# A gated mix of two attentions: x taken in features-first from the host instead of being transposed on TensorE

## The chip, the core and the metric

The kernel runs on one core of a Trainium2 chip. The metric is the device time of one execution in microseconds (us). A difference of about 0.5% (10 us here) is what a measurement of this kernel can tell from no change.

## The reference, cut to what matters

```
x: 2048 x 512                                     # float32, one batch
g = sigmoid((x * gate_w).sum(-1))                 # one number per row of x
qA, kA, vA = x @ wq, x @ wk, x @ wv               # 32 heads of 16
qB, kB, vB = split(x @ wqkv)                      # 32 heads of 16
a = (local attention in 4 segments of 512 rows, causal,
     mixed by sigmoid(beta) with a linear-attention memory carried over the segments) @ wo
b = softmax(qB kB' / 4) vB @ B_wo                 # over all 2048 rows
out = g * a + (1 - g) * b
```

x is an operand of all six projections, which contract over its 512 features. TensorE contracts over partitions, so the projections need x with features on the partitions. Only the gate needs x with rows on the partitions.

## The kernel before, in words

The 2048 rows are cut into four chunks of 512 rows, and each chunk into four tiles of 128 rows. Each float32 operand of a projection is split into a rounded part ("hi", the tiles `xh`, `ws`, `wv`) on ScalarE and a rest ("lo", `xl`) on VectorE, and a projection of a tile or chunk is three products of four 128-deep matmuls each, 12 matmuls into one PSUM bank (`TERMS`, L253).

**The start (L642 to L686).** SyncE loads x in 16 tiles of 128 rows, 256 KB each, into an eight-slot buffer `RAW` (`load_x`, L159). `do_x` (L163) transposes a tile in four 128x128 pieces on TensorE, copies the PSUM bank to `xh` on ScalarE (L171), and subtracts on VectorE into `xl` (L172). `dot_gate` (L177) multiplies the same rows by `gate_w` on VectorE and sums them. Then come eight jobs `qk_job` (L274), two for each chunk: queries and keys of attention B for the first group of eight heads. A job ends with a copy on ScalarE (L286), a subtraction on VectorE (L289) and two stores of 256 KB each to DRAM on SyncE's queue (L295), whose DRAM side has the shape 8 x 16 x 512; the staging tile `st` has four buffers. The transposes of the next chunk stand between a chunk's first and second job in TensorE's order.

**The A value projection (L686 to L700).** Sixteen jobs `v_job("A", tt)` (L255), one for each row tile. ScalarE copies each result (L267) into one of two staging tiles `VS` that lie in `vb` and hold two jobs each; SyncE stores a staging tile when it is full (L269, 544 KB, 128 partitions wide: the "value stores" below, eight of them). Jobs 5 and 6 therefore wait for value store 1, jobs 9 and 10 for value store 3, and so on. PSUM has six banks in rotation here, so TensorE's job n needs the copy of job n - 6. Between the second and the third value store SyncE issues twelve loads of `beta`, which fetch single 4-byte elements (L184, L187). GpSimd's own queue loads weights (L234, L242) and fills constant rows from a tile `aux` in 256-byte pieces (L148) during this time. `do_gate` (L198) takes the sigmoid of the gate sums.

**The rest.** Sixteen blocks of A's query and key projections with the memory, the B value projection as filler (L722 to L805), then 32 iterations of scores, exponentials and products with the values (L905 to L939), and a tail.

Every engine works its instructions strictly in the order of the program text (`manual_schedule`, L43). The order on a DMA queue is the order of issue. SyncE's DMAs share eight semaphores in turn, so a DMA is issued only when the one issued eight places before it has landed.

Of the kernel before, what the change touches and what calls it, by code (L numbers as in the profile page):

```python
# [7 lines left out]
FT = mybir.dt.float32  # L8
# [3 lines left out]
AF = mybir.ActivationFunctionType  # L12
OP = mybir.AluOpType
# [5 lines left out]
E = 16  # L19
SEQ = 2048  # L20
DM = 512
C = 512
NC4 = SEQ // C
NT = SEQ // 128
# [6 lines left out]


@with_exitstack
def gated_mix_kernel(ctx, tc, x, wq, wk, wv, wo, beta, wqkv, wob, gate_w, out):
    nc = tc.nc
    xr = x.rearrange("b s d -> (b s) d")
    outr = out.rearrange("b s d -> (b s) d")
# [13 lines left out]
    ident = P.tile([128, 128], FT, name="ident")  # L51
# [19 lines left out]
    X = proj.enter_context(tc.tile_pool(name="proj", bufs=1))  # L71
    XL = [X.tile([128, 4, C], FR, name=f"xl{c}") for c in range(NC4)]
# [22 lines left out]
    def misc():  # L95
        return bank(mode["misc"])
# [12 lines left out]
    def rot(key, lst):  # L109
        i = cnt.get(key, 0)  # L110
        cnt[key] = i + 1
        return lst[i % len(lst)]

    def raw_buf():
        i = cnt.get("raw", 0)
        cnt["raw"] = i + 1
        return RAWV[i if i < 6 else 6 + (i - 6) % 8]


    def identity():  # L120
        jp = X.tile([128, C], FT, name="phi0").bitcast(I32)[:, :128]
        nc.gpsimd.iota(jp, pattern=[[1, 128]], base=0, channel_multiplier=-1)
        nc.vector.tensor_scalar(ident, jp, 0.0, None, op0=OP.is_equal)

        for j in range(2):
            r = slice(64 * j, 64 * j + 64)
            for n in range(2):
                o = 64.0 * (n - j)
                nc.vector.tensor_scalar(crows[r, n], jp[r], o, None, op0=OP.is_equal)
                nc.vector.tensor_scalar(cmask[r, n], jp[r], o, MASK, op0=OP.is_gt, op1=OP.mult)  # L130

    def constants():
# [21 lines left out]
    def load_gate():  # L154
        nc.sync.dma_start(gw, bass.AP(tensor=gate_w.tensor, offset=gate_w.offset, ap=[[0, 128], [1, DM]]))

    XR = {}

    def load_x(tt):  # L159
        XR[tt] = RAW[:, tt % 8]  # L160
        nc.sync.dma_start(XR[tt], xr[tt * 128:(tt + 1) * 128, :])

    def do_x(tt):  # L163
        c, tl = divmod(tt, 4)
        xt = XR.pop(tt)
        b = misc().rearrange("p (k t) -> p k t", k=4)
        for k in range(4):
            nc.tensor.transpose(b[:, k, :], xt[:, k * 128:(k + 1) * 128], ident)
        hi = XH[c][:, :, tl * 128:(tl + 1) * 128]
        lo = XL[c][:, :, tl * 128:(tl + 1) * 128]  # L170
        nc.scalar.activation(hi, b, AF.Copy)  # L171
        nc.vector.tensor_tensor(lo, b, hi, op=OP.subtract)  # L172
        XG[tt] = xt

    XG = {}

    def dot_gate(tt):  # L177
        scr = W.tile([128, DM], BF, name="scr", bufs=1)
        nc.vector.scalar_tensor_tensor(scr, XG.pop(tt), 1.0, gw, op0=OP.mult, op1=OP.mult,
                                       accum_out=gate[:, tt:tt + 1])  # L180
# [17 lines left out]
    def do_gate():  # L198
        e = X.tile([128, NT], FT, name="ge")
        nc.scalar.activation(e, gate, AF.Exp, scale=-1.0)  # L200
        nc.vector.tensor_scalar(e, e, 1.0, None, op0=OP.add)
        nc.vector.reciprocal(gate, e)
# [17 lines left out]
    def split(hi, lo, raw):  # L220
        nc.scalar.activation(hi, raw, AF.Copy)
        nc.vector.tensor_tensor(lo, raw, hi, op=OP.subtract)

    def wcols(kd, w):
        if kd == "A":
            return (wq, wk, wv)[w], 0
        return wqkv, w * DM

    WR = {}

    def load_wv(kd, k):
        src, c0 = wcols(kd, 2)
        WR[k] = raw_buf()
        nc.gpsimd.dma_start(WR[k], src[k * 128:(k + 1) * 128, c0:c0 + DM])  # L234

    def split_wv(k):
        split(WV[0][:, k, :], WV[1][:, k, :], WR.pop(k))

    def load_w_raw(kd, g, w):
        src, c0 = wcols(kd, w)  # L240
        raw = raw_buf().rearrange("p (k c) -> p k c", k=4)
        nc.gpsimd.dma_start(raw, src.rearrange("(k p) c -> p k c", p=128)[:, :, c0 + g * 128:c0 + (g + 1) * 128])  # L242
        return raw

    def load_w(kd, g):
        WR[kd, g] = [load_w_raw(kd, g, w) for w in range(2)]

    def split_w(n, kd, g, ws=(0, 1)):
        for w in ws:
            split(WS[n][w][0], WS[n][w][1], WR[kd, g][w])  # L250
# [4 lines left out]
    def v_job(kd, tt):  # L255
        c, tl = divmod(tt, 4)
        b = misc()
        n = 0
        for xi, wi in TERMS:
            for k in range(4):  # L260
                lhs = (XH, XL)[xi][c][:, k, tl * 128:(tl + 1) * 128]
                nc.tensor.matmul(b, lhs, WV[wi][:, k, :], start=n == 0, stop=n == 11)  # L262
                n += 1
        if tl % 2 == 0:
            rot("vs", VS)
        vs = VS[(cnt["vs"] - 1) % 2]
        nc.scalar.activation(vs[:, tl % 2, :, :E], b.rearrange("p (h e) -> p h e", h=H), AF.Copy)  # L267
        if tl % 2:
            nc.sync.dma_start(VD[kd][tt * 128 - 128:(tt + 1) * 128].rearrange("(a t) g h e -> t a (g h e)", a=2),  # L269
                              vs.rearrange("p a h e -> p a (h e)"))  # L270
# [70 lines left out]
    def load_vm(g, c):  # L341
        PHI[g, "v", c] = X.tile([128, 4, 8, E + 1], FT, name="vm", bufs=2)
        v_src(PHI[g, "v", c], "A", g, c)
# [37 lines left out]
    def load_q(u):  # L381
        kd, qd, c = UN[u]
        load_qk(q_of(u), kd, 0, qd, c)
# [249 lines left out]
    def todo(fn, *a):  # L633
        return lambda: fn(*a)
# [4 lines left out]
    def s_tasks(u):  # L639
        return [todo(s_a, u, *t) for t in ST_A] if u < 32 else [todo(s_b, u, *t) for t in ST_B]  # L640

    for tt in range(4):  # L642
        load_x(tt)
    identity()
    load_w("B", 0)
    for tt in range(4, 8):
        load_x(tt)
    load_gate()
    constants()

    for tt in range(3):
        do_x(tt)
    split_w(0, "B", 0, (0,))
    do_x(3)
    split_w(0, "B", 0, (1,))
    def dots(tt):
        for t in (tt, tt + 1):
            dot_gate(t)
            if t + 8 < NT:
                load_x(t + 8)  # L660

    dots(0)
    dots(2)
    for c in range(NC4):
        for w in range(2):
            qk_job(0, "B", 0, w, c)
            if c + 1 < NC4:
                if w == 0:
                    for t in range(4):
                        do_x(4 * c + 4 + t)  # L670
                dots(4 * c + 4 + 2 * w)
            elif w == 0:
                split_wv(3)
        if c == 1:
            for k in range(4):
                load_wv("A", k)
        if c == 2:
            for k in range(3):
                split_wv(k)
# [5 lines left out]
        nc.vector.memset(t.bitcast(FT), 0.0)  # L685
    for tt in range(NT):  # L686
        v_job("A", tt)
        if tt == 2:
            split_w(0, "A", 0)
            do_gate()  # L690
        if tt == 3:
            load_beta()
        if tt in (7, 9, 11):
            load_wv("B", (tt - 7) // 2)
        if tt == NT - 1:
            load_vm(0, 0)
            load_kb(0)
            load_q(32)
        if ax:
            set_aux(*ax.pop(0))  # L700
# [21 lines left out]
    for blk in range(16):  # L722
        g, c = divmod(blk, 4)
# [9 lines left out]
        n = blk + 1 + (c == 2)  # L733
# [261 lines left out]
```

## Time and profile before

| | |
|---|---|
| device time, three runs | 1976.98, 1983.9 and 1985.88 us; median 1983.9 |
| the profiled execution | span 1976.0 us from first to last instruction; its own time is not listed apart, the lowest of the three runs is 1.0 us above the span |
| TensorE (PE) busy | 98% of the span |
| VectorE (DVE) busy | 83% |
| ScalarE (ACT) busy | 73% |
| GpSimd (POOL) busy | 13% |

Busy time counts an engine's instructions, not the waits between them. PEld is the weight load of a matmul, SPq the instruction by which SyncE issues a DMA, POOL with a DMA instruction the same on GpSimd's queue. A row of a timeline has the start in us from the begin of the span, the duration of the group, the engine, the line, the operation with its output and inputs, and in brackets how long the engine had been idle and what ended that. "PEclk" is the share of its clock that TensorE was granted. q1 is the queue of the DMAs that SyncE issues, q0 that of GpSimd's.

### The profile page before, as it was taken

What the parts mean: (1) busy time and instruction counts of PE and PEld (TensorE: products, weight loads), DVE (VectorE), ACT (ScalarE), POOL (GpSimd) and SP (SyncE); (2) the same over time, 40 slices, a digit from 0 to 9 for tenths busy, and PEclk for the clock granted to TensorE, in tenths of its full rate; (3) what the DMA queues carried; (4) which work ended last, traced back from release to release, by engine and by line L of the source; (5) the groups of instructions that cost most, each with busy time, mean ns of one, the idle gap of its engine ahead of it and who ended that gap; (6) DMA issues with size and microseconds to landing.
All of it is one profiled execution on the core that took longest, in us unless ns stands there. A gap on an engine that the chain in (4) does not pass through costs nothing.

```text
span 1976.0 us, 43643 instructions
## 1 busy us (share of the span) xinstructions
PE 1944.8 (98%) x17517; PEld 945.6 (48%) x17517; DVE 1630.3 (83%) x1825; ACT 1435.7 (73%) x2703; POOL 257.5 (13%) x474
## 2 busy tenths in 40 slices
PE   8999999999999999999999999999999999999999
PEld 6887777434344344444444444444444444444435
DVE  6135665899999999999999999999999999999942
ACT  3233332688888888888888888888888888888884
POOL 2200000011210101111010101010101010101012
PEclk9999999999999999999999999999999999999999
DMA  6766656644443444344445353444344444444111
GB/s 205 172 209 183 191 186 173 152 111 114 97 114 88 103 86 103 86 114 86 114 85 112 86 113 86 114 86 114 86 108 91 96 102 87 102 90 103 48 51 57
DMA packets 162742, 222.49 MB, mean 113 GB/s; under 512 B 39260, under 2 KB 89452, under 8 KB 156780
## 3 DMA queue, kind: packets, MB, share of 16 engines
q1 hardware_dynamic: 159596, 211.70, 44.0%
q0 software_dynamic: 2944, 8.00, 2.1%
q8 instruction: 138, 2.26, 0.5%
q14 instruction: 64, 0.52, 0.1%
HBM read 148.21 MB, written 68.16 MB: 109 GB/s over the span
## 4 chain that ended last, share of the span: by engine, by line
PE 90%; DMA 3%; DVE 2%; ACT 2%; issue 1%; SPq 1%; ACTq 0%; DVEq 0%
PE pvb L525 31%; PE tb L503 17%; PE sbk L449 12%; PE mb L503 8%; PE tb L279 3%; PE tb L591 2%; PE mb L279 2%; PE sbk L427 2%; PE pvb L279 2%; PE tb L262 2%; DVE mxb L451 1%; ACT raw L509 1%; PE mb L591 1%; PE mb L262 1%; PE sbk L431 1%
## 5 line engine op out<-in xcount | busy, mean ns | idle before, releaser
L451 DVE TENSOR_REDUCE mxb<-sbk 128x2 f32<-128x1024 f32 x1024 | 1226.1, 1222 | 36.6 <-PE sbk L449 32.4
L509 ACT ACTIVATE raw<-tb 128x512 f32<-128x512 f32 x1557 | 888.2, 598 | 163.1 <-PE tb L503 90.7
L525 PE MATMUL pvb<-raw,vb 128*17 128x256 f32 (+1 forms) x8072 | 639.4, 388 | 0.0
L509 ACT ACTIVATE raw<-mb 128x512 f32<-128x512 f32 x780 | 466.4, 598 | 76.5 <-PE tb L503 44.8
L503 PE MATMUL tb<-qb,xh 64*128 64x512 f32 x872 | 330.8, 496 | 1.7 <-ACT raw L509 1.7
L525 PEld LDWEIGHTS pvb<-raw,vb 128*17 128x17 f32 x8072 | 134.4, 95 | 341.7 <-issue 336.6
L449 PE MATMUL sbk<-xh,qb 64*128 64x512 f32 x1344 | 283.1, 398 | 2.0 <-DMA xh<-dB 0.8
L503 PE MATMUL mb<-qb,xh 64*128 64x512 f32 x445 | 219.6, 494 | 0.0
L503 PEld LDWEIGHTS tb<-qb,xh 64*128 64x128 f32 x872 | 124.4, 183 | 188.1 <-issue 91.4
L512 POOL TENSOR_SCALAR_AFFINE_SELECT raw<-raw 128x256 f32<-128x256 f32 (+1 forms) x320 | 116.1, 363 | 700.1 <-ACT raw L509 692.3
L503 PE MATMUL tb<-qb,kb 64*128 64x512 f32 x471 | 176.3, 496 | 1.4 <-DMA qb<-mr 0.8
L435 DVE TENSOR_REDUCE mx<-sbk 128x2 f32<-128x768 f32 (+1 forms) x128 | 139.8, 1092 | 43.1 <-PE sbk L431 37.1
L449 PE MATMUL sbk<-kb,qb 64*128 64x512 f32 x704 | 150.6, 406 | 1.2 <-DVE mxb L451 1.1
L449 PEld LDWEIGHTS sbk<-xh,qb 64*128 64x128 f32 x1344 | 137.9, 186 | 7.3 <-DVE mxb L451 3.5
L503 PEld LDWEIGHTS mb<-qb,xh 64*128 64x128 f32 x445 | 81.3, 183 | 86.6 <-issue 48.0
L503 PE MATMUL mb<-qb,kb 64*128 64x512 f32 x233 | 115.4, 495 | 0.7 <-DVE st L289 0.7
L565 POOL TENSOR_TENSOR o<-o,d 128x512 f32<-128x512 f32 x31 | 39.8, 1283 | 562.6 <-DMA d<-rd 281.6
L503 PEld LDWEIGHTS tb<-qb,kb 64*128 64x128 f32 x471 | 66.0, 183 | 98.4 <-issue 52.5
L525 PE MATMUL pvb<-raw,va 128*17 128x256 f32 (+2 forms) x1280 | 94.7, 383 | 5.8 <-ACT pvs L534 5.8
L427 PE MATMUL sbk<-ka,qa 64*128 64x256 f32 (+3 forms) x512 | 86.8, 346 | 1.2 <-ACT raw L509 1.2
L503 PE MATMUL tb<-qa,ka 64*128 64x384 f32 (+3 forms) x340 | 79.2, 372 | 0.0
L449 PEld LDWEIGHTS sbk<-kb,qb 64*128 64x128 f32 x704 | 71.6, 185 | 12.6 <-issue 6.5
(273 smaller groups left out, 1790.7 us busy)
## 6 DMA issues: line engine op xcount, KB each, us to landing
xh<-dB SPq DMA_DIRECT2D x38, 512.0 KB
vb<-vdB SPq DMA_DIRECT2D x16, 1088.0 KB
dB<-st SPq DMA_DIRECT2D x64, 256.0 KB
dA<-st SPq DMA_DIRECT2D x64, 256.0 KB
pd<-pvs SPq DMA_DIRECT2D x64, 256.0 KB
kb<-dB SPq DMA_DIRECT2D x22, 512.0 KB
xh<-dB SPq DMA_DIRECT2D x38, 256.0 KB
qb<-dB SPq DMA_DIRECT2D x64, 128.0 KB
```

What stands on the lines that cost most here:

```text
L262: nc.tensor.matmul(b, lhs, WV[wi][:, k, :], start=n == 0, stop=n == 11)
L279: nc.tensor.matmul(b, WS[ws][w][wi][:, k, :], (XH, XL)[xi][c][:, k, :], start=n == 0, stop=n == 11)
L427: nc.tensor.matmul(b[:, j, c0:c0 + n], q_of(u)[r, p, i * 128:(i + 1) * 128], k_of(u, p)[r, :n], start=True, stop=False)
L435: nc.vector.tensor_reduce(m[:, :, p, i], b[:, :, :n], axis=AX.X, op=OP.max)
L449: nc.tensor.matmul(b[:, j], q_of(u)[r, p, i * 128:(i + 1) * 128], k_of(u, p)[r, kc * C:(kc + 1) * C], start=True, stop=True)
L451: nc.vector.tensor_reduce(MXB[u][:, :, p, i, kc], b, axis=AX.X, op=OP.max)
L503: nc.tensor.matmul(bs[j][:, c0:c0 + w], k_of(u, h // 2)[r, 128 * it:128 * it + 128], q_of(u)[r, h // 2, q0:], start=True, stop=True)
L509: nc.scalar.activation(pt, bs[j], AF.Exp, scale=SCALE)
L512: nc.gpsimd.affine_select(out=m, in_=m, pattern=[[1, 128]] if n < 2 else [[0, 2], [1, 128]], compare_op=OP.is_ge, fill=0.0, base=0, channe ...
L525: nc.tensor.matmul(PVB[32 * h:32 * h + E + 1, q0 + lo:q0 + hi], vt[:, it, 4 * q + h, :], pt[:, lo:hi], start=it == 0 and lo == 0, stop=it ...
L565: nc.gpsimd.tensor_tensor(o, o, d, op=OP.mult)
L591: nc.tensor.matmul(b, (AT["oh"], AT["ol"])[oi][:, g, a], (AT["wh"], AT["wl"])[wi][:, g, a], start=n == 0, stop=n == 11)
```

## The change

The host also hands over x with features first (`xt`, 512 x 2048). The kernel loads a chunk of it as `[128 features, 4, 512 rows]`, 1 MB, into one half of `RAW`; chunk 0 in four DMAs of 256 KB, each later chunk in one. The split goes from SBUF: ScalarE copies `RAW` to `xh`, VectorE subtracts to `xl`. The 64 transposes and their 16 visits of a PSUM bank are gone from TensorE.

The rows of x are still loaded, for the gate alone, into four tiles whose names are otherwise used later (`phi0`, `phi1`, `om`, `pk`), one row tile per load, each load after the sum of the tile four places before it. Rows 0 to 3 are issued after the load of chunk 2, rows 4 to 9 one by one after the stores of jobs 3 to 8, row 10 ahead of the first value store, rows 11 and 12 behind it, 13 behind the second, 14 behind the `beta` loads, 15 behind the third; `do_gate` moves from job 3 to job 11 there. The load of chunk 3 comes after the stores of job 1. The load of the query weights of the first job goes to ScalarE's queue, that of the key weights stays on GpSimd's. The constants on VectorE and the identity come after the first loads.

```
-    def do_x(tt):
-        c, tl = divmod(tt, 4)
-        xt = XR.pop(tt)
-        b = misc().rearrange("p (k t) -> p k t", k=4)
-        for k in range(4):
-            nc.tensor.transpose(b[:, k, :], xt[:, k * 128:(k + 1) * 128], ident)
-        hi = XH[c][:, :, tl * 128:(tl + 1) * 128]
-        lo = XL[c][:, :, tl * 128:(tl + 1) * 128]
-        nc.scalar.activation(hi, b, AF.Copy)
-        nc.vector.tensor_tensor(lo, b, hi, op=OP.subtract)
-        XG[tt] = xt
+    XS = [RAW[:, 4 * (c % 2):4 * (c % 2) + 4] for c in range(NC4)]
+
+    def load_xt(c, ks=slice(0, 4)):
+        nc.sync.dma_start(XS[c][:, ks], xt.rearrange("(k p) t -> p k t", p=128)[:, ks, c * C:(c + 1) * C])
+
+    def split_x(c, ks):
+        split(XH[c][:, ks], XL[c][:, ks], XS[c][:, ks])
+
     def load_x(tt):
-        XR[tt] = RAW[:, tt % 8]
-        nc.sync.dma_start(XR[tt], xr[tt * 128:(tt + 1) * 128, :])
+        t = X.tile(*(([128, C], FT), ([128, C], FT), ([128, 4, 8, E], FT), ([128, 4, 128], FT))[tt % 4],
+                   name=("phi0", "phi1", "om", "pk")[tt % 4])
+        XG[tt] = t if tt % 4 < 2 else t.rearrange("p i h e -> p (i h e)" if tt % 4 == 2 else "p i r -> p (i r)")
+        nc.sync.dma_start(XG[tt], xr[tt * 128:(tt + 1) * 128, :])
...
+    WR["B", 0] = [load_w_raw("B", 0, w, (nc.scalar, nc.gpsimd)[w]) for w in range(2)]
+    for k in range(4):
+        load_xt(0, slice(k, k + 1))
+    load_xt(1)
+    load_gate()
+    identity()
+    split_w(0, "B", 0, (0,))
+    for k in range(4):
+        split_x(0, slice(k, k + 1))
+    split_w(0, "B", 0, (1,))
+    load_xt(2)
+    for tt in range(4):
+        load_x(tt)
+    constants()
...
+    def dot(tt):
+        if 0 <= tt < NT:
+            dot_gate(tt)
+            if tt + 4 < NT:
+                load_x(tt + 4)
+
     for c in range(NC4):
         for w in range(2):
             qk_job(0, "B", 0, w, c)
             if c + 1 < NC4:
                 if w == 0:
-                    for t in range(4):
-                        do_x(4 * c + 4 + t)
-                dots(4 * c + 4 + 2 * w)
+                    for n in range(2):
+                        split_x(c + 1, slice(2 * n, 2 * n + 2))
+                    if c == 0:
+                        load_xt(3)
             elif w == 0:
                 split_wv(3)
+            dot(2 * c + w - 2)
...
     for tt in range(NT):
         v_job("A", tt)
+        dot(tt + 6)
         if tt == 2:
             split_w(0, "A", 0)
+        if tt == 10:
             do_gate()
```

`split` is the helper that the weights already used (L220): one ScalarE copy, one VectorE subtraction.

More of the change, by code (lines that the diff above doesn't have):

```diff
@@ L33, in gated_mix_kernel @@
 @with_exitstack
-def gated_mix_kernel(ctx, tc, x, wq, wk, wv, wo, beta, wqkv, wob, gate_w, out):
+def gated_mix_kernel(ctx, tc, x, wq, wk, wv, wo, beta, wqkv, wob, gate_w, xt, out):
     nc = tc.nc
@@ L155, in load_gate @@
         nc.sync.dma_start(gw, bass.AP(tensor=gate_w.tensor, offset=gate_w.offset, ap=[[0, 128], [1, DM]]))
-    XR = {}
-    def load_x(tt):
-        XR[tt] = RAW[:, tt % 8]
-        nc.sync.dma_start(XR[tt], xr[tt * 128:(tt + 1) * 128, :])
-    def do_x(tt):
-        c, tl = divmod(tt, 4)
-        xt = XR.pop(tt)
-        b = misc().rearrange("p (k t) -> p k t", k=4)
-        for k in range(4):
-            nc.tensor.transpose(b[:, k, :], xt[:, k * 128:(k + 1) * 128], ident)
-        hi = XH[c][:, :, tl * 128:(tl + 1) * 128]
-        lo = XL[c][:, :, tl * 128:(tl + 1) * 128]
-        nc.scalar.activation(hi, b, AF.Copy)
-        nc.vector.tensor_tensor(lo, b, hi, op=OP.subtract)
-        XG[tt] = xt
-    XG = {}
+    XS = [RAW[:, 4 * (c % 2):4 * (c % 2) + 4] for c in range(NC4)]
[3 more added lines that the diff above has]
+        split(XH[c][:, ks], XL[c][:, ks], XS[c][:, ks])
+    XG = {}
+    def load_x(tt):
+        t = X.tile(*(([128, C], FT), ([128, C], FT), ([128, 4, 8, E], FT), ([128, 4, 128], FT))[tt % 4],
+                   name=("phi0", "phi1", "om", "pk")[tt % 4])
+        XG[tt] = t if tt % 4 < 2 else t.rearrange("p i h e -> p (i h e)" if tt % 4 == 2 else "p i r -> p (i r)")
+        nc.sync.dma_start(XG[tt], xr[tt * 128:(tt + 1) * 128, :])
     def dot_gate(tt):
@@ L237, in split_wv, with load_w_raw @@
         split(WV[0][:, k, :], WV[1][:, k, :], WR.pop(k))
-    def load_w_raw(kd, g, w):
+    def load_w_raw(kd, g, w, eng=None):
         src, c0 = wcols(kd, w)
         raw = raw_buf().rearrange("p (k c) -> p k c", k=4)
-        nc.gpsimd.dma_start(raw, src.rearrange("(k p) c -> p k c", p=128)[:, :, c0 + g * 128:c0 + (g + 1) * 128])
+        (eng or nc.gpsimd).dma_start(raw, src.rearrange("(k p) c -> p k c", p=128)[:, :, c0 + g * 128:c0 + (g + 1) * 128])
         return raw
@@ L640, in s_tasks @@
         return [todo(s_a, u, *t) for t in ST_A] if u < 32 else [todo(s_b, u, *t) for t in ST_B]
+    WR["B", 0] = [load_w_raw("B", 0, w, (nc.scalar, nc.gpsimd)[w]) for w in range(2)]
[9 more added lines that the diff above has]
+    load_xt(2)
     for tt in range(4):
         load_x(tt)
[L644 to L648, printed above, removed]
-    constants()
[L651 to L663, printed above, removed]
+    constants()
+    def dot(tt):
[3 more added lines that the diff above has]
+                load_x(tt + 4)
     for c in range(NC4):
@@ L986 @@
         args.append(nc.dram_tensor(f"in_{name}_dram", a.shape, _mybir.dt.from_np(a.dtype), kind="ExternalInput").ap())
+    a = _np.ascontiguousarray(inputs["A_x"][0].T)
+    arrays["in_xt_dram"] = a
+    args.append(nc.dram_tensor("in_xt_dram", a.shape, _mybir.dt.from_np(a.dtype), kind="ExternalInput").ap())
     for i, (shape, dtype) in enumerate(_OUTS):
```

## The prediction

> **What bounds the kernel now.** I read the page first, then the busy time by stage, then the start and the value projection row by row, last the DMA queues.
>
> ```profile
> span 1976.0 us, 43643 instructions
> ...
> PE 1944.8 (98%) x17517; PEld 945.6 (48%) x17517; DVE 1630.3 (83%) x1825; ACT 1435.7 (73%) x2703; POOL 257.5 (13%) x474
> ...
> PE 90%; DMA 3%; DVE 2%; ACT 2%; issue 1%; SPq 1%; ACTq 0%; DVEq 0%
> ```
>
> TensorE fills 98% of the span and 90% of the chain that ended last. Each engine works in a fixed order, so a microsecond that TensorE saves early arrives at the end, if nothing takes it back on the way.
>
> ```profile
> core 0: us, PE busy (x) PEld busy (x) DVE busy (x) ACT busy (x) POOL busy (x), PEclk, DMA share, GB/s
> 0.00:10.30 10.30, 4.14 (x16) 3.00 (x16) 4.81 (x15) 4.21 (x7) 6.33 (x19) 1.00 0.81 272
> 10.30:43.90 33.60, 30.95 (x144) 25.36 (x145) 25.55 (x58) 12.87 (x24) 0.22 (x1) 0.95 0.60 192
> 43.90:88.60 44.70, 44.70 (x195) 36.31 (x194) 4.81 (x8) 8.73 (x17) 17.08 (x31) 1.00 0.74 162
> ```
>
> The change lies in the first two stages, ahead of 43.9 us. The third, the A value projection, keeps TensorE full (44.70 of 44.70); after it the code is the same. So the question is when TensorE leaves the third stage. (About 0.5%, 10 us, is what a measurement of this kernel can tell from no change.)
>
> ```profile
> ACT vb L267 <- DMA vdA<-vb: 27.1, 6, 13.9
> ...
> PEld mb L262 <- ACT vb L267: 0.2, 1, 0.2
> ```
>
> These two waits say that it only just stays full: ScalarE's copies wait 27.1 us for value stores to land, and once TensorE itself waits for such a copy.
>
> ```profile
> 65.64 1.09 ACT L267 ACTIVATE vb<-sbk 128x512 f32<-128x512 f32 x2 [8.34 <-DMA vdA<-vb]
> ...
> 82.26 0.60 ACT L267 ACTIVATE vb<-mb 128x512 f32<-128x512 f32 x1 [13.91 <-DMA vdA<-vb]
> ...
> 82.95 1.38 PE L262 MATMUL mb<-wv,xh 128*128 128x512 f32 x5
> ```
>
> This is the place: the copy of job 9 waits until 82.26 for the third value store, and TensorE's job 15, which needs that PSUM bank, starts at 82.95, 39.05 us after the stage began. All six banks are used up: **any later landing of the third store, measured from the stage's start, stops TensorE**.
>
> **The change part by part.**
>
> ```profile
> 10.33 3.66 PE L279 MATMUL sbk<-xh,ws 128*128 128x512 f32 x8 [0.69 <-ACT xh L171]
> 13.83 1.09 PE L279 MATMUL sbk<-xl,ws 128*128 128x512 f32 x4
> 14.76 0.60 PE L168 MATMUL sbk<-ident,raw 128*128 128x128 f32 x4
> ...
> 16.42 2.10 PE L279 MATMUL pvb<-xh,ws 128*128 128x512 f32 x8
> ...
> 19.28 2.02 PE L279 MATMUL sbk<-xh,ws 128*128 128x512 f32 x8
> ...
> 33.05 0.66 PE L168 MATMUL tb<-ident,raw 128*128 128x128 f32 x4 [2.63 <-DMA raw<-in_A_x_dram]
> ...
> 34.12 3.66 PE L279 MATMUL pvb<-xh,ws 128*128 128x512 f32 x8
> ```
>
> *Removed.* Four tiles of transposes take 1.66 us of TensorE (14.76 to 16.42), three chunks' worth 5.0 us; a wait of 2.6 us for rows of x and the slow clock behind it (8 matmuls in 3.66 us instead of 2.02, so 1.64 us) go too. A job of 12 matmuls takes 2.8 us (16.42 to 19.28).
>
> ```profile
> 8.49 0.60 ACT L171 ACTIVATE xh<-mb 128x512 fp32r<-128x512 f32 x1 [2.34 <-PE mb L168]
> ...
> 8.99 0.62 ACT L221 ACTIVATE ws<-va 128x512 fp32r<-128x512 f32 x1
> ...
> 9.73 0.68 DVE L222 TENSOR_TENSOR ws<-va,ws 128x512 fp32r<-128x512 f32 x1
> ...
> 14.44 0.69 DVE L179 SCALAR_TENSOR_TENSOR scr<-raw,gw 128x512 bf16<-128x512 f32 x1 [2.82 <-DMA gw<-in_gate_w_dram]
> ```
>
> ```profile
> 3.50:8.50 5.00, 3.06 (x12) 2.29 (x12) 1.49 (x3) 1.20 (x3) 3.86 (x12) 1.00 0.96 328
> ```
>
> *Chunk 0.* Four loads and two weights are the same bytes as now, so the fourth piece lands at about 8.5; split from SBUF by rows of this kind, 0.62 and 0.68 us, its lo is there at 9.8. Job 1 does eight of its matmuls by then, and with the slow clock ends near 12.6, against 14.9. Without any wait the other seven would end at 12.6 + 7 x 2.8 = 32.
>
> *Chunk 3 comes late.* The load of chunk 2 joins the queue behind `gate_w` (landed 14.4). Behind it stand rows 0 to 3, job 1's stores, and only then chunk 3. At 328 GB/s a megabyte takes 3.2 us: 14.4 + 3.2 + 3.2, stores with their constant 3.4 (rate below), + 3.2 = 27.4. Half a split more, at most 1.24 on ScalarE: job 7 starts near 28.5 instead of 26.6, and the value stage starts at **about 34** instead of 43.9. So TensorE is 9.6 us ahead there (bounds 7 to 12: chunk 3 three later, or no wait).
>
> *Moving the query weights to ScalarE's queue* I cost at nothing: the sum of bytes ahead of chunk 0 is what it was. Bounds: 0.6 us either way, the 0.62 of one split. The gate sums on VectorE keep their number (16 x 0.69) and have cover: VectorE is busy 4.81 of 44.7 us in the value stage.
>
> *What takes the gain back: the queue.* x is now read twice, 4.2 MB more, and the copies of rows stand in SyncE's queue among the stores.
>
> ```profile
> q1 hardware_dynamic: 821, 1.56, 51.6%
> ...
> dB<-st SPq DMA_DIRECT2D x4, 256.0 KB
> ```
>
> ```profile
> 14.00:16.00 2.00, 2.00 (x16) 1.78 (x16) 1.50 (x5) 1.04 (x3) 0.00 (x0) 1.00 0.00 0
> 16.00:38.00 22.00, 19.37 (x97) 15.87 (x95) 18.30 (x41) 8.04 (x16) 0.00 (x0) 0.92 0.66 203
> 38.00:44.00 6.00, 6.00 (x28) 4.85 (x27) 4.54 (x10) 3.29 (x6) 0.22 (x1) 1.00 0.45 146
> ```
>
> The first fence is the queue from 30 to 38 us, where it holds only jobs' stores: its share stands at half, 1.56 MB in 8 us, 195 GB/s. I read this as eight of the sixteen DMA engines full and eight idle. A store of 0.26 MB then takes 1.34 us of those eight. A row tile, spread over all sixteen, takes them half of 1.34, **0.67 us**.
>
> By the Trainium skill, "DMA: Bandwidth & Descriptors", section "Why a DMA increments its semaphore by 16 and not by 1", a DMA runs on the largest number of engines up to 16 that divides the outermost dimension on both sides; a store whose outer dimension is 8 thus gets eight, which agrees with the 51.6%. By the same page's fabric figure of 435 GB/s a row tile would take 0.60 us, an estimate; fifteen of them 9.0 us instead of the 10.0 below.
>
> ```profile
> 50.55 7.20 SPq L269 DMA_DIRECT2D vdA<-vb  x2
> 57.79 8.65 SPq L184 DMA_DIRECT2D gh<-in_A_beta_dram  x4
> 66.49 8.42 SPq L187 DMA_DIRECT2D nq<-in_A_beta_dram  x8
> 75.02 16.32 SPq L269 DMA_DIRECT2D vdA<-vb  x6
> ```
>
> The first value store is issued at 50.55, just behind the last jobs' stores; the copy behind it starts at 65.64. The `beta` loads then hold SyncE's queue for 17 us, and the third value store leaves at 75.02 and lands at 82.2. All of it hangs on when the eight engines have worked off what stands ahead: 16 stores, and in the new order 15 row tiles more (0 to 14) ahead of the third value store: 15 x 0.67 = **+10.0 us**. Against it stands idle time that the new order fills: 2.0 (14 to 16 us), 0.8 (38 to 44: share 0.45 of 0.516), and a part of the 22 us between. There 203 GB/s make 4.47 MB: eight row tiles (2.10 MB, 5.4 us), constants (0.13 MB, 0.7 us) and 2.24 MB of stores (11.5 us), 17.6 us; 4.4 are left. So 10.0 - 7.2 = +2.8. If a row tile among stores costs the eight engines as much as a load at 328 GB/s takes, 0.80 us, it is 12.0 - (2.0 + 0.8 + 3.4) = +5.8. I have nothing to choose between the two and take the middle: the third store lands **4.3 us later** than now.
>
> GpSimd's queue adds a term that no row gives alone; the queues from 66 to 75 us:
>
> ```profile
> q0 software_dynamic: 473, 0.83, 58.7%
> q1 hardware_dynamic: 941, 0.05, 6.2%
> ```
>
> From 66 to 75 us it takes 58.7% of the engines, 5.3 us, while the `beta` elements need 6.2%: now this work is hidden beside them. It starts after the last `wv` split, so 9 us earlier in the new kernel, and may fall ahead of the `beta` loads: between 0 and +5.3. It is paced by its own landings, which tells for the lower end; I take +1. It could help, too, where `beta` then has the engines to itself: -1 at the lower end.
>
> *Waits added.* Each row load waits on SyncE's queue for the gate sum four places before it, and behind it stand stores and the `beta` loads; the sums wait for rows of the same queue, so their time is in the sum above. ScalarE's step of `do_gate`, now after the copy of job 11, waits for the sum of row 15; that row is issued ahead of the fourth value store, for which the copy of job 11 waits anyway, so 0, at most one sum, 0.7.
>
> *Sum.* Third store +5.3; TensorE's job 15 starts at 88.2 instead of 82.9. TensorE comes to that point at 34 + 39 = 73 and waits 15 us in all (some of it earlier, at job 11 for the first store), so the clock falls, as behind the wait of 2.6 us at 33: +1.6 for the next matmuls. Together **+6.9 us**. What is late next, stores four to eight, has room: all six are issued within 16.3 us (75.02), and TensorE works two jobs, 5.6 us, for each one that it needs. From there the order is the same, and the shift stays.
>
> Against the profiled execution that is a span of 1976.0 + 6.9 = 1982.9. The median of the runs stands 7.9 above the span of before, so 1983.9 + 6.9 = **1990.8 us**.
>
> **The rivals.**
>
> *The gain is kept.* The flat half share could be a queue that moves little at a time; row tiles would slip into its free half and cost nothing, and the third store would land by 73. Then the start's 9.6 us stay: 1974.3. For it: 0.00 from 14 to 16 and 0.45 from 38 to 44 show room. Against it: a load of 0.26 MB reaches 328 GB/s when it is alone, so the queue can fill all engines, and it needs the third store 9 us sooner than now with more work ahead of it. By the rule of the Trainium skill on the number of engines the half share is eight full ones, which speaks against this rival too.
>
> *GpSimd's fills fall wholly ahead of `beta`* (slower). One mechanism: fills in pieces of 256 bytes take the engines from SyncE's queue, here from 54 to 62 us:
>
> ```profile
> q0 software_dynamic: 226, 0.50, 82.8%
> q1 hardware_dynamic: 168, 0.36, 13.0%
> ```
>
> They leave it 13%. If all of the fills and weights, 5.3 us more, run while stores and rows queue, and a row tile costs the 0.80 us, the third store lands 5.8 + 5.3 = 11.1 later; with the clock +12.7, 1996.6.
>
> ```profile
> 45.05 0.76 POOL L242 DMA_DIRECT2D raw<-in_A_wq_dram  x1 [0.30 <-issue]
> ```
>
> GpSimd starts this 1.2 us after the value stage begins, so near 35 in the new kernel. It decides from the point where at that time four or more jobs' stores (2.7 us each) still wait; by my working it is four to five, so this is near.
>
> *Less is taken back*: the lower end for rows (+2.8) and for the fills (-1), clock 1.6: +3.4, 1987.3. I count it with the forecast.
>
> **How the numbers follow.** Forecast (shift of 0 to +9.9) 0.47; fills ahead, from +9.9 up, 0.30; the gain kept 0.17, of which 0.12 lies beyond 9.9 (chunk 3 without a wait gives up to 12); a small gain of 0 to 5 us 0.06. So faster by over 0.5% 0.12, within 0.5% 0.47 + 0.05 + 0.06 = 0.58, slower by over 0.5% 0.30. The range reaches from a gain of 7 (1977), which leaves out most of the first rival, to +16 (2000), the second with two more stalls of 1.6 us; the likeliest case alone is 1984 to 1994.
>
> **What would show it.** Right: no rows of L168; TensorE's first value job near 34; in the value stage two waits of TensorE for ScalarE's copies, the longer one at job 15, with PEclk below 1; the wait of those copies for value stores well above 27 us; a DMA share at or above 0.9 from 3 to 45 us. Wrong: a value stage as full as now would mean that rows cost the stores nothing; a first value job later than 40 that chunk 3, not the queue behind it, is the trouble; and a shift that appears only after 100 us would be a mechanism that I have not named.

## The result and the profile after

| | before | after |
|---|---|---|
| median, seven runs each, side by side | 1977.66 us (1976.2 to 1985.88) | 1989.82 us (1987.93 to 1991.38) |
| ratio after / before, 95% interval | | 1.0047 (1.0035 to 1.0059), +9.3 us (+6.9 to +11.7) |
| span of the profiled execution | 1976.0 us | 1988.7 us |

After is slower, by about the bound of 0.5%. The medians themselves are 12.2 us apart, outside that interval: the seven times of before lie in two groups, 1976.2 to 1977.66 and 1981.2 to 1985.88, and its median is the highest of the lower group. The forecast was a shift of +6.9 us and a time of 1990.8 us.

The page of after, its span, the busy time, and the chain that ended last by engine:

```profile
span 1988.7 us, 43499 instructions
...
PE 1942.9 (98%) x17453; PEld 942.0 (47%) x17453; DVE 1629.5 (82%) x1819; ACT 1434.8 (72%) x2697; POOL 256.0 (13%) x473
...
PE 89%; DMA 3%; ACT 3%; DVE 2%; issue 1%; SPq 1%; ACTq 0%; DVEq 0%
```

TensorE has 64 instructions less, but only 1.9 us less of busy time. Ahead of the value stage it saves 8.2 us (35.31 us busy up to 44.12 us in before, 27.12 up to 35.77 in after). In the value stage the same 194 matmuls take 5.0 us more (49.44 instead of 44.46), at a granted clock of 0.86 instead of 1.00, and the remaining 1.3 are lost later. The busy time fell and the span rose by 12.7: what came in is waiting. The stages of after:

```profile
core 0: us, PE busy (x) PEld busy (x) DVE busy (x) ACT busy (x) POOL busy (x), PEclk, DMA share, GB/s
0.00:10.30 10.30, 3.16 (x6) 1.99 (x7) 5.24 (x16) 4.62 (x7) 1.40 (x6) 1.00 0.79 264
10.30:34.00 23.70, 22.20 (x84) 17.15 (x84) 15.78 (x26) 11.75 (x17) 4.18 (x12) 0.93 0.85 295
34.00:43.90 9.90, 9.90 (x45) 8.03 (x44) 5.50 (x12) 2.11 (x4) 5.49 (x10) 1.00 0.84 241
43.90:100.00 56.10, 43.55 (x168) 34.62 (x167) 8.76 (x24) 10.48 (x20) 11.74 (x22) 0.85 0.69 167
```

Between 10.3 and 34 us TensorE is busy 22.20 of 23.70 us, and from 35.8 us on it is already in the value projection. In the last stretch it works 43.55 of 56.1 us at a clock of 0.85, where before it was full (44.70 of 44.70). Its waits and starts there, first by what was waited for, then row by row:

```profile
ACT vb L263 <- DMA vdA<-vb: 40.8, 6, 20.8
...
PE tb L258 <- ACT vb L263: 7.4, 1, 7.4
...
PE sbk L258 <- ACT vb L263: 5.1, 1, 5.1
```

```profile
28.05 0.74 PE L275 MATMUL tb<-xh,ws 128*128 128x512 f32 x2 [1.29 <-ACT xh L217]
...
35.77 2.02 PE L258 MATMUL mb<-wv,xh 128*128 128x512 f32 x8
...
71.09 3.78 PE L258 MATMUL tb<-wv,xh 128*128 128x512 f32 x8 [7.42 <-ACT vb L263]
...
90.35 3.78 PE L258 MATMUL sbk<-wv,xh 128*128 128x512 f32 x8 [5.13 <-ACT vb L263]
...
97.76 2.02 PE L275 MATMUL tb<-xh,ws 128*128 128x512 f32 x8
```

The value stage starts at 35.77 against 44.12, 8.35 us ahead. TensorE then stands twice for ScalarE's copies of results (jobs 11 and 15), 7.42 and 5.13 us, each time with a slow clock behind it (eight matmuls in 3.78 us). Job 15 starts at 90.35 against 82.95, and the first matmul behind the stage at 97.76 against 88.58: **the lead of 8.35 us has become a lag of 9.2**. The copies' wait for value stores grew from 27.1 to 40.8 us. SyncE's queue shows why:

```profile
40.89 6.77 SPq L171 DMA_DIRECT2D phi<-in_A_x_dram  x1
47.75 3.36 SPq L171 DMA_DIRECT2D om<-in_A_x_dram  x1
51.33 4.94 SPq L265 DMA_DIRECT2D vdA<-vb  x1
...
68.54 4.24 SPq L180 DMA_DIRECT2D gh<-in_A_beta_dram  x4
72.83 8.29 SPq L183 DMA_DIRECT2D nq<-in_A_beta_dram  x8
81.22 1.04 SPq L171 DMA_DIRECT2D om<-in_A_x_dram  x1
82.36 0.38 SPq L265 DMA_DIRECT2D vdA<-vb  x1
...
89.70 1.09 ACT L263 ACTIVATE vb<-sbk 128x512 f32<-128x512 f32 x2 [14.56 <-DMA vdA<-vb]
```

The first value store leaves at 51.33, where it left at 50.55 before, though TensorE is 8.35 us earlier; row loads stand in front of it. The third leaves at 82.36 instead of 75.02, and the copy that waits for it, that of job 9, starts at 89.70 instead of 82.26.

Later, a place that before has too (it waits 3.00 and 0.83 us there, at 342 and 349 us) takes a little more:

```profile
353.79 1.12 PE L323 MATMUL pvb<-ident,om 128*128 128x128 f32 x4 [2.57 <-DVE om L316]
357.92 0.79 PE L499 MATMUL tb<-qb,kb 64*128 64x512 f32 x2 [3.01 <-DMA qb<-mr]
```

By the same instruction TensorE is 8.5 to 9.2 us behind from 98 to 347 us, then for a moment only 3.7 (at 351 us, when before has had its wait of 3.00 us and after has not had its own), 11.3 from 361 us on, and 12.6 at the end.

### The profile page after: what moved, and what is told of

Same layout as the page of the kernel before. It is cut to its first block, busy times and chain, and to the rows that moved or that the text cites. A ratio compares the mean times of both kernels' runs of the same rounds, so it can differ in the third digit from the quotient of the medians.

```text
span 1988.7 us, 43499 instructions
## 1 busy us (share of the span) xinstructions
PE 1942.9 (98%) x17453; PEld 942.0 (47%) x17453; DVE 1629.5 (82%) x1819; ACT 1434.8 (72%) x2697; POOL 256.0 (13%) x473
## 4 chain that ended last, share of the span: by engine, by line
PE 89%; DMA 3%; ACT 3%; DVE 2%; issue 1%; SPq 1%; ACTq 0%; DVEq 0%
PE pvb L521 31%; PE tb L499 17%; PE sbk L445 12%; PE mb L499 8%; PE tb L275 4%; PE tb L587 2%; PE pvb L275 2%; PE sbk L423 2%; PE mb L275 2%; ACT raw L505 1%; PE mb L587 1%; DMA phi<-in_A_x_dram 1%; DVE mxb L447 1%; PE sbk L427 1%; PE tb L258 1%
## 5 line engine op out<-in xcount | busy, mean ns | idle before, releaser
L505 ACT ACTIVATE raw<-mb 128x512 f32<-128x512 f32 x780 | 466.7, 598 | 76.7 <-PE tb L499 40.8
```

The source lines that it names most:

```text
L505: nc.scalar.activation(pt, bs[j], AF.Exp, scale=SCALE)
```

## The experiments

"Shift" is the start of a TensorE instruction in the experiment less the start of the same instruction in the first profile of before; "the ratio" is to before, with its 95% interval. Beside these runs the median of before was 1978.0 to 1982.8 us, so the ratios compare better than the times. The theory: row loads among the stores put the third value store late, and with it TensorE.

**1. Before reads x a second time.** Sixteen row tiles are loaded at after's places and read by nobody.

```
+    def load_x2(tt): ... nc.sync.dma_start(t, xr[tt * 128:(tt + 1) * 128, :])
+            if c > 0: load_x2(2 * c + w + 2)     # among the jobs' stores
         v_job("A", tt)
+        load_x2(tt + 10)
```

> The kernel before, with its transposes, and sixteen more loads of row tiles at the places where the changed kernel has its row loads; nobody reads them, so no gate sum is waited for. Theory (the second reading of x alone pushes the value stores back): the third value store lands 5 to 8 us later than 82.2, TensorE waits about as long at job 15 and runs 3.5 us at the slow clock: 6 to 9 us slower than before, 1984 to 1987 us. Rival (the rows cost nothing by themselves; what costs is that the value stage starts earlier than the queue can follow, or the waits on gate sums): within 2 us of the kernel before, 1976 to 1980 us.

Measured: 1990.14 us, ratio 1.0044 (1.0028 to 1.0059). The third value store leaves at 83.10 (before 75.02), and TensorE stands once, at the place foretold:

```profile
90.86 3.78 PE L270 MATMUL mb<-wv,xh 128*128 128x512 f32 x8 [8.86 <-ACT vb L275]
```

The shift behind the stage is +10.7. The time lies above the 1984 to 1987 that were expected; by the ratio the loss is 8.7 us, within the expected 6 to 9. No gate sum is waited for here, so the loss does not need those waits. The second reading alone costs what the whole change costs; that the transposes are gone gives nothing that lasts.

**2. After without rows 4 to 15.** The gate of these rows is then not that of the reference.

```
-                load_x(tt + 4)
+                XG[tt + 4] = XK[tt % 4]     # rows 0 to 3 again
```

> The changed kernel, with only rows 0 to 3 of x loaded for the gate; the gate sums of tiles 4 to 15 are made from these four again, so twelve row loads of 256 KB and the waits on SyncE's queue before them are left out (the gate of later rows is then not that of the reference). Theory (rows in the queue push the value stores back): the first value store lands before 62 us and the third before 76, TensorE waits at neither job 11 nor job 15 or under 2 us in all, and the 8 us by which the value stage starts earlier stay: 1968 to 1973 us. Rival (the element loads of beta and GpSimd's fills, which now start while stores still wait, are what holds the third store, rows or not): job 15 still waits 3 us or more, 1979 us or above.

Measured: 1973.78 us, ratio 0.9962 (0.995 to 0.9974). TensorE has no wait in the value stage, and the third store leaves early:

```profile
68.09 15.04 SPq L265 DMA_DIRECT2D vdA<-vb  x6
```

The shift, -6.6 at the stage's start, is -7.3 at 322 us and -4.0 at 380 us. The mechanism holds; the time is just above the 1968 to 1973 that were expected, whose sum left out the loss at that late place.

**3. The banks turned.** The removed visits of PSUM banks turn the rotation by four; here they are turned back, to see whether that is behind the late place.

```
+    for _ in range(4):
+        misc()
     WR["B", 0] = [load_w_raw("B", 0, w, (nc.scalar, nc.gpsimd)[w]) for w in range(2)]
```

> The changed kernel, with the rotation of PSUM banks turned by four places at the start, so that every job from the value stage on has the bank that it has in the kernel before. Nothing else differs. After the value stage the changed kernel is 9.0 us behind and at the end 12.6 us; between 340 and 365 us the two differ in which job waits. Theory (the later loss comes from the turn of the banks, not from the queue): waits between 340 and 365 us as in the kernel before (one of 3 us before a projection, 0.8 before scores), the value stage unchanged (waits of 7.4 and 5.1 us), 2 to 4 us faster than the changed kernel: 1986 to 1988 us. Rival (the later loss is another wait for a DMA that the shift brings with it): no difference, 1989 to 1991 us.

Measured: 1988.55 us, ratio 1.0044 (1.0029 to 1.0059). Two waits in the stage again (5.64 and 5.68 us), +8.3 behind it and +12.5 at 380 us: the banks are not the cause. The time lies between the two that were expected.

**4. `beta` on GpSimd's queue, early.**

```
-            nc.sync.dma_start(gh[:, g:g + 1], ...      # and nq
+            nc.gpsimd.dma_start(gh[:, g:g + 1], ...    # issued behind the A value weights
```

> The changed kernel, with its twelve loads of beta issued on GpSimd's queue behind the wv loads (near 15 us) instead of on SyncE's between the second and the third value store. Theory (the value stores come late because SyncE's queue is full; the beta loads are one part of what stands ahead of the third): the third store lands near 76 us instead of 89.6, the wait of 5.1 us at job 15 and its slow clock go, the wait of 7.4 us at job 11 for the first store stays; about 6.5 us faster than the changed kernel, 1983 us (1981 to 1986). Rival (the bytes of the rows alone fill the queue, the beta loads hide beside them): job 15 still waits 4 us or more, 1988 to 1991 us.

Measured: 1991.78 us, ratio 1.0049 (1.003 to 1.0067). A miss, with a cause of its own: the twelve loads of single elements, issued from 14.9 us on, ran beside chunk 3's load, which was issued at 16.5 us and could be split only from 39.31 on:

```profile
40.42 3.88 PE L275 MATMUL tb<-xh,ws 128*128 128x512 f32 x8 [14.02 <-ACT xh L217]
```

So this run says nothing of `beta` in the value stage. The next asks again.

**5. `beta` behind the value stores.**

```
-        if tt == 3:
-            load_beta()
...
             load_q(32)
+            load_beta()                       # the four for gh, behind the stage
...
+        if 2 <= blk < 10:
+            load_beta((), (blk - 2,))         # the eight for nq, one at a time
```

> After, with the twelve beta loads moved behind all value stores (four behind the loads that follow the value stage, eight one at a time in the next stage). Theory (rows put the stores late, and the beta loads then hold the third store): the first store still leaves near 51 and TensorE still waits about 7 us at job 11, but the third store leaves near 70 instead of 82.4, the wait of 5.1 us at job 15 and its slow clock go, the shift after the value stage falls from +9 to about +2.5: 1983. Rival (the rows alone hold the queue; what beta gives up is filled by rows and stores): the third store gains less than 4 us and the time stays within 3 us of after, 1987 to 1990.

Measured: 1986.51 us, ratio 1.0023 (1.0006 to 1.0041). SyncE's queue:

```profile
66.33 1.53 SPq L171 DMA_DIRECT2D om<-in_A_x_dram  x1
69.73 0.38 SPq L267 DMA_DIRECT2D vdA<-vb  x1
```

The third store leaves at 69.73 (expected 70), the wait at job 15 is gone, the one at job 11 stays with 7.28 us, and the shift behind the stage is -1.0. Up to there the theory holds, with 3.5 us more than it asked for. But the moved loads charge their price later: a wait of 4.42 us for `om` at 132 us, and +6.5 at 239 us. (The ten times of this kernel lie between 1978.86 and 1992.69; the profiled execution took 1989.23.) Both parts of the queue count, rows for job 11, rows and `beta` for job 15.

**6. Rows behind the third value store.** The same bytes in all; the gate sums of these rows and `do_gate` come later to match.

```
-            dot(2 * c + w - 2)
+            if 2 * c + w < 6:
+                dot(2 * c + w - 2)            # sums of rows 0 to 3 alone, no loads here
...
+        if 5 <= tt < 11:
+            load_x(2 * tt - 6)
+            load_x(2 * tt - 5)
```

> After, with rows 4 to 15 loaded behind the third value store (in pairs, from value job 6 on) and not among the first job stores; the same bytes in all. Theory (what costs is what stands ahead of the first three value stores, not the second reading as such): the stage starts about 8 us ahead, the third store leaves near 68 as with four rows, no wait over 1 us of TensorE in the value stage, shift -4 to -7: 1972 to 1976. Rival (bytes: the engines are full through the whole stage, so the rows stop stores four to eight instead): waits of 5 us or more at a later job, 1980 or above.

Measured: 1983.51 us, ratio 1.0018 (1.0006 to 1.0029). The third store leaves at 67.76 (expected 68), but TensorE waits at job 15 and again behind the stage:

```profile
77.02 3.58 PE L258 MATMUL sbk<-wv,xh 128*128 128x512 f32 x8 [3.88 <-ACT vb L263]
...
92.38 1.54 PE L258 MATMUL mb<-wv,xh 128*128 128x512 f32 x3 [2.43 <-ACT wv L217]
```

The shift is -4.3 at 88 us and +1.2 at 98 us. Nearer to the rival: the loss is smaller than in after and comes later.

**7. The same, and `beta` on GpSimd's queue behind all its fills.**

```
-                load_x(tt + 4)                # as in 6
...
         if tt in (7, 9, 11):
             load_wv("B", (tt - 7) // 2)
+        if tt == 11:
+            load_beta()                       # nc.gpsimd.dma_start
...
+        if blk == 1:
             do_beta()                         # one block later
```

> After, with rows 4 to 15 behind the third value store as in the run with rows behind, and with the twelve beta loads on GpSimd's queue behind all its fills. Theory (the third value store is late through what SyncE works off ahead of it: rows first, beta then): with neither ahead of it, the third store leaves when its copy is done, near 52 instead of 82.4; no wait of TensorE over 1 us in the value stage; the start stays 9 to 10 us ahead until about 90, and 2 to 4 us of it go at 335 to 365 us as in the other runs: span 1969 to 1973, median 1971 to 1977, below before. Rival (the engines themselves are short of time in this stretch): a wait of TensorE of 4 us or more at a later job, or the split of the B value weights late at 90 us, and 1979 or more.

Measured: 1983.44 us, ratio 1.0006 (0.9993 to 1.0019). TensorE is full through the whole value stage, 9.8 us ahead until 84 us; then

```profile
92.38 1.83 PE L258 MATMUL mb<-wv,xh 128*128 128x512 f32 x3 [7.93 <-ACT wv L217]
```

ScalarE's last copies wait 11.80 and 3.12 us for value stores that now stand behind rows and `beta` elements, so it splits the B value weights late. All of the lead is lost in one stop. The third store does not leave at 52 as expected but at 58.58: its copy waited for the first store, which landed by 57. Theory and rival are each half right: the order decides where TensorE stops, and with x read twice there is not enough room in this stretch for any of the orders tried to be free of a stop.

**8. Rows 4 to 15 from GpSimd's queue**, at the same places of the program.

```
-                load_x(tt + 4)
+                load_x(tt + 4, nc.gpsimd)
```

> After, with rows 4 to 15 loaded from GpSimd's queue at the same places of the program; the same bytes, but SyncE no longer waits for a gate sum ahead of a store. Theory (the rows' share of the engines while half of them hold the stores is what costs): the first value store leaves at 45 or later instead of 41 without rows, TensorE still waits 5 us or more in the value stage, 1984 to 1992. Rival (SyncE's waits for gate sums ahead of the value stores are what costs: 6.8 us at 40.9 and 3.4 us at 47.8): the first value store leaves near 41, the third near 68, no wait over 2 us, 1972 to 1979.

Measured: 1979.83 us, ratio 1.0006 (0.9993 to 1.0019). The first value store leaves at 45.01, the third at 71.66; TensorE waits 2.27 us for a split and 3.32 us at job 15. Between theory and rival: by the ratios (1.0006 against 1.0047) the same bytes cost some 8 us less. What changed is seen in the DMA view of 40 to 55 us, of after and then of this run:

```profile
DMA packets 1127, 2.30 MB, mean 154 GB/s; under 512 B 207, under 2 KB 207, under 8 KB 1127
...
q0 software_dynamic: 430, 0.99, 67.0%
q1 hardware_dynamic: 697, 1.32, 32.0%
```

```profile
DMA packets 1571, 3.82 MB, mean 255 GB/s; under 512 B 184, under 2 KB 184, under 8 KB 1570
...
q0 software_dynamic: 596, 1.92, 56.6%
q1 hardware_dynamic: 974, 1.90, 35.8%
```

The engines are nearly full in both (99% and 92%), but in after GpSimd's queue, weights and fills in 256-byte pieces, holds two thirds of them and moves 0.99 MB, less than SyncE's queue moves in one third. With rows in GpSimd's queue the fills come later: the first is issued at 45.61 instead of 37.28 us. The run changes two things at once (SyncE no longer waits with its stores for row loads, and the fills come later) and does not part them.

**9. The jobs' stores in images of 128 rows**, in after and in before. These are the stores that I took to fill eight of sixteen engines.

```
+            if (kd, g) == ("B", 0):
+                QKD[kd, w, g] = [D.tile([8 * E, SEQ], FT, ...) for a in range(2)]
...
+                nc.sync.dma_start(QKD[kd, w, g][a][:, c * C:(c + 1) * C], st[:, a].bitcast(FT))
```

> After, with the stores of the first eight projection jobs (hi and lo of group 0 of the B branch) written to images of 128 rows of their own, so that the outer dimension in DRAM is 128 instead of 8; the loads of these images later become six or eight instead of four. Theory (these stores fill half the engines, 1.34 us each; in the new form 0.67): the DMA share from 30 to 38 us exceeds 0.85 while a queue stands, 16 stores are worked off 10 us sooner, the first value store leaves near 41 to 44 instead of 51.3, the third near 70 instead of 82.4, waits of TensorE in the value stage 2 us or less in all, start 9 to 11 ahead of before: 1972 to 1980. Rival (the queue is paced by something else, say bytes or the waits for gate sums): first value store still later than 48, waits of 5 us or more, 1985 to 1992.

> The same images of 128 rows in the kernel before. Theory: its stop of 0 to 4.5 us at job 15 goes (third value store near 65 instead of 75), and the copies' wait of 27.1 us for value stores shrinks below 15; no more, since TensorE was full otherwise: 1974 to 1979, ratio 0.996 to 1.000. Rival (the stores' form does not matter): 1979 to 1982, ratio 0.999 to 1.001, with the copies' wait above 24 us.

Measured: after so changed 1997.7 us, ratio 1.0103 (1.0085 to 1.0121); before so changed 1997.68 us, ratio 1.0102 (1.0085 to 1.0118). The queue from 30 to 38 us of the first:

```profile
DMA packets 1270, 2.43 MB, mean 303 GB/s; under 512 B 141, under 2 KB 141, under 8 KB 1268
...
q1 hardware_dynamic: 1220, 2.21, 83.3%
```

Before had a flat 51.6% and 1.56 MB there, after 66.2% and 1.88 MB. The first value store leaves at 38.79 instead of 51.33, the third at 68.78. So the half-full engines were real, and the rival falls for the queue. This agrees with the rule of the Trainium skill, "DMA: Bandwidth & Descriptors", "Why a DMA increments its semaphore by 16 and not by 1", that the outermost dimension sets the number of engines. But in after the stop at job 15 stays, where 2 us at most were expected:

```profile
75.89 3.68 PE L262 MATMUL sbk<-wv,xh 128*128 128x512 f32 x8 [4.53 <-ACT vb L267]
```

In the kernel before TensorE does not stop in the value stage, but the third store leaves at 69.28 (expected 65) and the copies still wait 23.4 us for value stores (expected below 15). The times were missed because the loads of these images, six or eight where four were, cost later: SyncE needs 17.4 us between the first two `vm` loads (84.39 and 101.77), where run 8 needs 6.8, and after so changed TensorE waits 7.04 us for `om` at 129 us and more at 346 to 356 and at 679 to 735 us. In this form the images do not pay.

**10. Gate sums from the features-first copy.** No rows at all; VectorE multiplies hi and lo by `gate_w` and adds up the feature blocks, TensorE sums over partitions.

```
+        nc.vector.scalar_tensor_tensor(a, s[c][:, k], gc[:, k:k + 1], a, op0=OP.mult, op1=OP.add)
...
+        nc.tensor.matmul(b[:, tt:tt + 1], ACC[c][:, tl * 128:(tl + 1) * 128], one, start=True, stop=True)
```

> After without any load of rows: VectorE forms the gate products from the features-first halves in the value stage (32 operations of about 0.7 us where it is idle), and TensorE adds the 128 partitions up in 16 small matmuls (about 2 to 4 us) ahead of job 15. Theory: with x read once the stores land early, TensorE does not wait in the value stage, chunk 3 comes without a wait of 2.5 us, so the value stage starts 8 to 10 us ahead of before; less the 2 to 4 us of matmuls: 1970 to 1976, below before by 4 to 10. Rival: the features-first load costs by itself (order of the queue, splits), then no better than 1980.

Measured: 1978.45 us, ratio 0.9987 (0.9974 to 1.0001): 0.6% better than after by the ratios, and not to be told from before. The value stage starts 10.6 us ahead and the lead stays to job 15:

```profile
73.07 1.95 PE L675 MATMUL sbk<-one,phi 128*128 128x1 f32 x16
74.88 1.03 PE L675 MATMUL sbk<-one,om 128*128 128x1 f32 x8
75.77 1.03 PE L675 MATMUL sbk<-one,pk 128*128 128x1 f32 x8
76.66 3.27 PE L258 MATMUL tb<-wv,xh 128*128 128x512 f32 x8
```

The sums then take 3.6 us of TensorE and leave a slow clock behind them, -10.1 becomes -4.7, and small waits at 125 us and later take it to -2.0. By the ratio 2.6 us are gained, less than the 4 to 10 that were expected. Reading x once, features first, is worth 10 us at job 15; the sums over rows for the gate are what has to be paid for.

**11. Before, profiled again.**

> The unchanged kernel before, profiled a second time. Open is why after and all variants so far lose another 2.3 to 4 us on TensorE between 335 and 365 us, which the first profile of before does not show. Theory: that first profile (1976.98 us; before ranges from 1975.8 to 1986.2) was a lucky execution, and a second one shows the waits for dB, om or qb<-mr transfers there too: the time at which TensorE reaches 380 us then differs from the first by 1 us or more, with waits of over 4 us in all between 335 and 365 us (3.8 in the first). Rival: the loss belongs to the second reading; then the two profiles of before agree within 0.5 us there.

Measured: 1982.08 us, span 1980.4, and it differs where I had not looked:

```profile
85.84 3.66 PE L262 MATMUL mb<-wv,xh 128*128 128x512 f32 x8 [2.32 <-ACT vb L267]
```

Before itself stops at job 15 in this execution, +4.5 us behind the stage. Its third store left at 75.82, 0.8 later than in the first profile. From 322 to 380 us it loses 0.6 us against the first profile, less than all but one of the other kernels, so in the sum the rival nearly holds there. Wait by wait it does not: the waits are 2.25 and 3.12 us, where the first profile has 3.00 and 0.83. After's wait of 3.01 us for `qb<-mr` is thus one that before can have too.

## Why the prediction came out as it did

**Right: the direction of the shift and its mechanism.** The transposes saved time only up to the value stage, and the second reading of x took it back through the third value store (runs 1, 2 and 5).

- *Chunk 0.* Job 1 was to end near 12.6; job 2's matmuls follow from 12.66 on.
- *Chunk 3.* Job 7 at 28.5 forecast, 28.05 measured. The value stage was to start at 34 and started at 35.77: I left out the slow clock behind the waits at job 7, the same 1.64 us that I had taken off the old kernel.
- *The queue.* Half-full engines: shown by run 9. The DMA share from 3 to 45 us was to be 0.9 or more and is 0.88. What the rows cost stands with the fills, next.
- *GpSimd's fills and weights: the step that was mis-sized.* I took +1 from a range of 0 to 5.3. The queues from the stage's start to the `beta` loads, and during these, before:

```profile
q0 software_dynamic: 290, 0.92, 52.4%
q1 hardware_dynamic: 600, 1.15, 30.8%
```

```profile
q0 software_dynamic: 758, 1.20, 57.6%
q1 hardware_dynamic: 1578, 1.08, 20.5%
```

and after, from 34 to 68.5 and from 68.5 to 82.4 us:

```profile
q1 hardware_dynamic: 2650, 5.06, 45.1%
q0 software_dynamic: 915, 1.92, 45.8%
```

```profile
q0 software_dynamic: 397, 0.83, 25.2%
q1 hardware_dynamic: 1416, 0.39, 12.8%
```

  The windows of before are 43.9 to 57.8 and 57.8 to 75 us. GpSimd's queue takes 0.524 x 13.9 = 7.3 us of all engines ahead of `beta` in before and 0.458 x 34.5 = 15.8 in after: +8.5. The `beta` loads start 10.75 us later (68.54 against 57.79), so 2.2 are left for the rows; 14 row tiles ahead of them (0 to 13) at 0.67, less the idle 7.2, make the same 2.2, near the lower of my two ends. In return `beta` passes in 12.7 us (68.54 to 81.22) instead of 17.2, -4.5. The fills are thus worth +4, and row 14 ahead of the third store +1.1. With the rows' +2.2 that is +7.3, which is what the third store shows (82.36 against 75.02); I had +5.3. The rival "fills ahead of `beta`" described what happened, but its price of +11.1 is too high: it has 5.8 for the rows, where 3.3 came (row 14 with them), and it left out what the `beta` loads get back. The split into rows and fills is arithmetic on these rows; no run moved the fills alone.
- *TensorE.* Job 15 at 88.2 forecast, 90.35 measured; the slow clock was to cost 1.6 and cost 1.8. I expected the longer wait at job 15; it is at job 11. That does not change the sum, since job 15 is bound by the third store either way.
- *Failed: "From there the order is the same, and the shift stays."* It grows from 9.0 us at 347 to 11.3 at 361 us, and to 12.6 by 1921 us. All other kernels lose 1.3 to 5.1 us between 322 and 380 us as well, but for run 10, which gains 0.7, and the second profile of before, which loses 0.6. Turning the banks back did not help. What decides there stays open.
- *The base.* I added my shift to the median of three runs, 1983.9. Over 7 to 25 runs before has medians of 1977.7 to 1982.8 on the chips of these runs. That the time came out within 1 us is luck: the shift was 2.4 us too small (6.9 against 9.3) and the base 3.4 us too high (1983.9 against 1989.82 - 9.3). Between the profiled executions the shift was to be 6.9 us and was 12.7. And the profile that I worked from was one in which the third store came just in time; run 11 shows the same program with a stop of 2.3 us at that very point. The text called this place one that TensorE only just passes, and still took its wait in before as exactly none.

## What to carry to other kernels

A transfer that is added has two prices: its own time on the engines, and what it lets pass ahead of the store that someone waits for; here the second was the larger one by the arithmetic above, and moving the loads moved the stop and at best made it smaller. Before you count a gain at a stage's start, find the store that ends the stage's last wait and work out when it lands in the new order. Profile the kernel before twice where a wait of zero sits at the edge: one execution does not tell whether the margin is there.

## What the runs showed of the hardware that was not expected

- One-column matmuls count as busy time and still left a lower clock behind them: in run 10 TensorE is busy 12.00 of 12.00 us from 74 to 86 us at a granted clock of 0.86, and the eight matmuls behind the 32 small ones take 3.27 instead of 2.02 us.
- Full DMA engines can move little: from 40 to 55 us they are 99% busy at 154 GB/s in after, where GpSimd's queue holds 67.0% and moves 0.99 MB, and 92% busy at 255 GB/s in run 8, where it holds 56.6% and moves 1.92 MB.
- Twelve loads of single elements on GpSimd's queue held up a 1 MB load on SyncE's queue so that TensorE waited 14.02 us (run 4).
- Two executions of one program differ by 0.8 us in the issue of a store and by 4.4 us in the span, since a stop of 2.3 us also brings the slow clock (run 11).
